# Decode attention on one core: value loads issued from ScalarE's queue instead of SyncE's

## The chip, the cores and the metric

The kernel runs on one core of a Trainium2 chip. The core has TensorE (PE, matrix products into PSUM), VectorE (DVE), ScalarE (ACT), GpSimd (POOL) and SyncE (SP), and 16 DMA engines that move data between the chip's memory and the core's SBUF. A load is issued by an instruction in the program of one engine, and each issuing engine has a DMA queue of its own. The metric is the device time of one execution in microseconds (us), lower is better.

## The reference

Two branches, A and B, of single-token attention over a cache of 4096 positions, 32 heads of 128, a batch of 2; all in float32. B uses A's input x. The branches are mixed by a gate.

```python
q = (x @ wq).reshape(B, Sq, Hq, Dh).transpose(0, 2, 1, 3)        # Sq = 1, Hq = 32, Dh = 128
scores = einsum("bhqd,bhkd->bhqk", q, k_cache) * Dh ** -0.5       # k_cache: 2 x 32 x 4096 x 128
p = softmax(scores, axis=-1)
o = einsum("bhqk,bhkd->bhqd", p, v_cache)
branch = o.transpose(0, 2, 1, 3).reshape(B, Sq, Hq * Dh) @ wo
...
g = sigmoid((x * gate_w).sum(-1, keepdims=True))
out = g * branch_A + (1 - g) * branch_B
```

## The kernel before

The work is cut into 32 units: branch (A, B), batch (2), and eight groups of four heads. A unit needs one tile of keys and one of values, each 128 partitions x 16384 float32 (8 MB): four heads times 32 stretches of 128 positions lie on the partitions. Units 0 to 15 belong to A, 16 to 31 to B. The query and output weights (`wq`, `wo`) of a branch are 8 MB each too, so all loads together are 68 such tiles: 2 wq, 32 keys, 32 values, 2 wo.

Keys, both wq, the values of the last unit (31) and the wo of B take turns in two buffers (`kt`). The values of units 0 to 30 and then the wo of A share one buffer (`vt`).

What a unit does:

- `scores(u)` on DVE: multiply the keys in place by the query (L182), then sum over each head's 128 elements (L183) into `sc`, of which there are two buffers. For units 0 and 16 both steps are done in halves, and the key is loaded in halves.
- `soft(u)`: DVE takes the maximum (L188 to L192, the last writes `nm`); ACT computes the exponentials, four pieces into `pr` (L197) and one into `pp` (L200). `pr` has one buffer.
- `values(u)`: 100 of 128 positions of a partition are weighted on PE, in 25 matmuls with `pr` (for the last unit 112). The other 28 are scaled in place on POOL (L220) and ACT (L222), added up on POOL (L227), and one more matmul with `heads` (L232 as well) takes their sum in. After every second unit ACT copies the result out (L236) and PE folds it into `gat` (L240). After every eighth (7, 15, 23, 31), `outputs` copies and multiplies once more, ending in the copy to `rows` on ACT (L253).

`project(n)` forms the queries of a branch on PE (L160, L168) from wq. `finish(n)` normalises `rows` on DVE and forms `on`; for A it stands behind `soft(16)`. At the end PE multiplies `on` by both wo (L299 to L309).

The order of instructions on each engine is the order in which the program writes them: the scheduler is manual. An engine runs its instructions strictly in that order, and a DMA issue waits in its engine's program like any other instruction, until the buffer that it fills is free. The loop is:

```python
for u in range(NU):
    scores(u)
    soft(u)
    ...                                  # finish("A") at u == 16
    load_k(u + 2 ...)                    # wq B at u == 14; value 31 at u == 30; wo B at u == 31
    ...                                  # at u == 15 also project("B"), load_k(17)
    values(u)
    ...                                  # wo A at u == 30
    load_v(u + 1)
```

So a key's load can be issued once VectorE has summed the unit two before, and a value's load once the last reader of the one value buffer, the matmul with `heads`, is done. Before the change, all loads but the two small ones into `raw` (x and gate_w, from ACT) are issued by SyncE, in this one sequence.

## Time and profile before

| | |
|---|---|
| median of 3 runs | 1325.07 us (1324.8 to 1325.48) |
| span of the profiled execution | 1324.0 us |
| read from memory | 570.43 MB |
| mean rate over the span | 431 GB/s |
| busy: PE, DVE, ACT, POOL | 407.2, 1129.4, 167.0, 369.0 us |

The profiled execution's own time is its span; it is 1.07 us under the median of the runs. In the page's lines, `Lnnn` is a line of the kernel, the engine and operation follow, then output<-input with shapes and the count; behind the bar stand the busy time, the mean in ns of one, and the idle time just before these instructions with what ended most of it. In a line of the timeline, the first number is the start and the second the duration in us; brackets give the engine's idle time before it and who ended it. SPq and ACTq are the issues of loads in the programs of SyncE and ScalarE; q1 is SyncE's DMA queue and q10 ScalarE's.

### The profile page before, as it was taken

To read this page: it belongs to the slowest core of one execution; us is meant where nothing else is said; L and a number is where in the kernel's file an instruction comes from. 1 tells how busy PE (TensorE), PEld (TensorE's weight loads), DVE (VectorE), ACT (ScalarE), POOL (GpSimd) and SP (SyncE) were. 2 spreads that over 40 slices of the span, in tenths; PEclk is the share of its full clock that TensorE was granted. 3 is DMA by queue.
4 is the path that set the end of the run, shared out by engine and by line. 5 is a ranking of instruction groups with operands and counts; after the bars stand their busy time and mean duration, and the time that the engine had idled before them with its cause. 6 is when DMAs were issued, how large, how long until landed. Compare 5 with 4: busy or idle time off the path is not lost.

```text
span 1324.0 us, 5510 instructions
## 1 busy us (share of the span) xinstructions
PE 407.2 (31%) x2092; PEld 98.9 (7%) x2092; DVE 1129.4 (85%) x191; ACT 167.0 (13%) x601; POOL 369.0 (28%) x145
## 2 busy tenths in 40 slices
PE   3132213233231323322442123332313332221356
PEld 1000000000000000000111000000000000000012
DVE  0999989889988888998369999899888889988860
ACT  0011101110110111011111101110111111011110
POOL 0033113333311333331132123333123333311350
PEclk9666556666656666665865566666556666655668
DMA  9999999999999999999999999999999999999998
GB/s 411 445 426 428 442 436 424 440 436 424 440 436 430 436 436 432 434 434 432 427 441 434 434 438 430 426 440 436 426 440 434 428 438 432 434 436 430 436 438 349
DMA packets 11124, 570.78 MB, mean 431 GB/s; under 512 B 1237, under 2 KB 1493, under 8 KB 1754
## 3 DMA queue, kind: packets, MB, share of 16 engines
q1 hardware_dynamic: 11092, 570.43, 99.6%
q8 instruction: 16, 0.26, 0.1%
q14 instruction: 10, 0.08, 0.0%
q10 hardware_dynamic: 6, 0.01, 0.0%
HBM read 570.43 MB, written 0.00 MB: 431 GB/s over the span
## 4 chain that ended last, share of the span: by engine, by line
DVE 50%; DMA 49%; PE 0%; issue 0%; SPq 0%; DVEq 0%
DVE sc L183 25%; DVE kt L182 25%; DMA kt<-in_A_k_cache_dram 25%; DMA kt<-in_B_k_cache_dram 22%; DMA kt<-in_B_wo_dram 3%; PE small L263 0%; DVE rm L188 0%; PE q L309 0%; SPq L89 0%; DVE tm L190 0%; DVE nm L192 0%; DVE rows L260 0%; SPq L79 0%; DVEq L183 0%; DVEq L336 0%
## 5 line engine op out<-in xcount | busy, mean ns | idle before, releaser
L182 DVE TENSOR_TENSOR kt<-kt,q 128x16384 f32<-128x16384 f32 (+1 forms) x34 | 551.3, 16215 | 131.9 <-DMA kt<-in_B_k_cache_dram 70.8
L183 DVE TENSOR_REDUCE sc<-kt 128x128 f32<-128x16384 f32 (+1 forms) x34 | 551.3, 16216 | 3.2
L232 PE MATMUL vp<-vt,pr 128*32 128x512 f32 x1550 | 258.7, 783 | 718.7 <-DMA vt<-in_A_v_cache_dram 379.5
L220 POOL TENSOR_TENSOR vt<-vt,pp 128x2560 f32<-128x2560 f32 x31 | 138.4, 4465 | 884.8 <-DMA vt<-in_A_v_cache_dram 468.3
L227 POOL TENSOR_TENSOR vt<-vt 128x1536 f32<-128x1536 f32 (+2 forms) x93 | 219.5, 2361 | 7.3
L222 ACT ACTIVATE vt<-vt,pp 128x128 f32<-128x128 f32 x248 | 75.9, 388 | 565.2 <-DMA vt<-in_A_v_cache_dram 291.3
L232 PEld LDWEIGHTS vp<-vt,pr 128*32 128x32 f32 x1550 | 68.2, 139 | 926.3 <-issue 920.7
L197 ACT ACTIVATE pr<-sc,nm 32x100 f32<-32x100 f32 (+1 forms) x128 | 59.9, 468 | 323.1 <-DVE nm L192 294.9
L232 PE MATMUL vp<-vt,heads 128*32 128x512 f32 x62 | 53.7, 965 | 108.9 <-POOL vt L227 108.9
L240 PE MATMUL gat<-vs,strip 128*32 128x512 f32 x32 | 29.8, 1032 | 11.0 <-ACT vs L236 11.0
L236 ACT ACTIVATE vs<-vp 128x512 f32<-128x512 f32 x16 | 9.6, 597 | 178.7 <-PE vp L232 178.7
L160 PE MATMUL small<-kt,xs 128*32 128x512 f32 x128 | 19.3, 758 | 17.0 <-DMA kt<-in_A_wq_dram 10.7
L197 ACT ACTIVATION_READ_ACCUMULATOR pr<-sc,nm 32x1 f32 x128 | 24.0, 187 | 0.0
L316 DVE COPY vs<-q 2x128 f32<-2x128 f32 x2 | 0.6, 282 | 23.5 <-PE q L309 23.5
L232 PEld LDWEIGHTS vp<-vt,heads 128*32 128x32 f32 x62 | 5.2, 130 | 137.1 <-POOL vt L227 137.1
L257 DVE RECIPROCAL rl<-rows 32x2 f32<-32x2 f32 x2 | 0.3, 148 | 15.8 <-ACT rows L253 15.8
L263 PE MATMUL small<-rows,deal 32*128 32x64 f32 x16 | 3.9, 418 | 29.0 <-DVE rows L260 29.0
L299 PE MATMUL q<-vt,on 128*2 128x512 f32 x64 | 9.1, 735 | 4.1 <-DMA vt<-in_A_wo_dram 4.1
L200 ACT ACTIVATE pp<-sc,nm 128x28 f32<-128x28 f32 (+1 forms) x32 | 10.2, 317 | 0.9
L188 DVE TENSOR_REDUCE rm<-sc 128x1 f32<-128x128 f32 x32 | 9.2, 286 | 1.1
L232 PE MATMUL vp<-kt,pr 128*32 128x512 f32 x56 | 7.7, 711 | 5.8 <-DMA kt<-in_B_v_cache_dram 5.8
L168 PE MATMUL q<-vs,spread 128*128 128x512 f32 x16 | 7.9, 618 | 3.0 <-ACT vs L164 3.0
(65 smaller groups left out, 88.1 us busy)
## 6 DMA issues: line engine op xcount, KB each, us to landing
kt<-in_A_k_cache_dram SPq DMA_DIRECT2D x2, 4096.0 KB, 35.7
kt<-in_B_k_cache_dram SPq DMA_DIRECT2D x2, 4096.0 KB, 38.3
kt<-in_B_wo_dram SPq DMA_DIRECT2D x1, 4096.0 KB
kt<-in_B_wo_dram SPq DMA_DIRECT2D x3, 1024.0 KB, 37.8
kt<-in_B_wo_dram SPq DMA_DIRECT2D x1, 512.0 KB, 40.4
vt<-in_A_v_cache_dram SPq DMA_DIRECT2D x16, 25.0
kt<-in_B_wo_dram SPq DMA_DIRECT2D x1, 256.0 KB, 40.5
kt<-in_B_wo_dram SPq DMA_DIRECT2D x2, 128.0 KB, 29.7
```

What stands on the lines that cost most here:

```text
L160: nc.tensor.matmul(r[h * QP:(h + 1) * QP], xs[:, c], cols[:, c, h, half * HG // 2:(half + 1) * HG // 2, :], start=c == 0, stop=c == KC - 1)
L182: nc.vector.tensor_tensor(k, k, q[:, None, :].to_broadcast([P, j - i, DH]), op=ALU.mult)
L183: nc.vector.tensor_reduce(sc[u][:, i:j], k, axis=AX.X, op=ALU.add)
L188: nc.vector.tensor_reduce(rm[:, 0:1], sc[u], axis=AX.X, op=ALU.max)
L197: nc.scalar.activation(w, sc[u][r, :spe].rearrange("p (c a) -> p c a", a=VC), AF.Exp, bias=nm[r], accum_out=lsum[r, g * HU + h:g * HU + h ...
L200: nc.scalar.activation(pp[u], sc[u][:, spe:], AF.Exp, bias=nm, accum_out=lpool[:, g:g + 1])
L220: nc.gpsimd.tensor_tensor(w[:, :m], w[:, :m], pp[u][:, :m, None].to_broadcast([P, m, DH]), op=ALU.mult)
L222: nc.scalar.activation(w[:, t], w[:, t], AF.Copy, scale=pp[u][:, t:t + 1])
L227: nc.gpsimd.tensor_tensor(x, x, y, op=ALU.add)
L232: nc.tensor.matmul(o[s * QP:(s + 1) * QP], w, x, start=not odd and c < STRIPS, stop=odd and c >= len(calls) - STRIPS)
L236: nc.scalar.activation(vs, o, AF.Copy)
L240: nc.tensor.matmul(gat[n, b][r:r + QP], strip, vs, start=True, stop=True)
```

## The change

The value loads of units 1 to 30 are issued from ScalarE. The loads of keys, of wq and wo, and of the values of units 0 and 31 stay on SyncE. The function's other lines, the buffers and the arithmetic are the same.

```diff
@@ -72,7 +72,8 @@
             vt[u] = big.tile([P, SLOTS, DH], F32, name="vt", bufs=1)
         else:
             vt[u] = big.tile([P, SLOTS, DH], F32, name="kt")
-        nc.sync.dma_start(vt[u], cache("v", u))
+        queue = nc.scalar if 0 < u < NU - 1 else nc.sync
+        queue.dma_start(vt[u], cache("v", u))
 
     def load_wq(n):
         wq[n] = big.tile([P, KC, H * DH], F32, name="kt")
```

Line numbers behind this place are one higher in the changed kernel.

First place: ScalarE's program around the end of a batch, units 6 and 7 and the beginning of 8, before the change. `vt_534` is the value tile of unit 6, `vt_592` of 7, `vt_665` of 8.

```order
L222 ACTIVATE vt_534<-vt_534,pp_549 128x128 x8
L197 ACTIVATE pr_88,lsum_90<-sc_594,nm_601 32x25x4 x4
L200 ACTIVATE pp_607,lpool_92<-sc_594,nm_601 128x28
L222 ACTIVATE vt_592<-vt_592,pp_607 128x128 x8
L236 ACTIVATE vs_652<-vp_553 128x512
L246 ACTIVATE vs_655<-gat_296 128x512
L253 ACTIVATE rows_663<-small_657 32x129
L197 ACTIVATE pr_88,lsum_90<-sc_667,nm_674 32x25x4 x4
L200 ACTIVATE pp_680,lpool_92<-sc_667,nm_674 128x28
```

The same place after the change:

```order
L223 ACTIVATE vt_534<-vt_534,pp_549 128x128 x8
L76 DMA vt_592<-in_A_v_cache_dram 128x16384
L198 ACTIVATE pr_88,lsum_90<-sc_594,nm_601 32x25x4 x4
L201 ACTIVATE pp_607,lpool_92<-sc_594,nm_601 128x28
L223 ACTIVATE vt_592<-vt_592,pp_607 128x128 x8
L237 ACTIVATE vs_652<-vp_553 128x512
L247 ACTIVATE vs_655<-gat_296 128x512
L254 ACTIVATE rows_663<-small_657 32x129
L76 DMA vt_665<-in_A_v_cache_dram 128x16384
L198 ACTIVATE pr_88,lsum_90<-sc_667,nm_674 32x25x4 x4
L201 ACTIVATE pp_680,lpool_92<-sc_667,nm_674 128x28
```

A value load now stands between the work on one unit's values and the exponentials of the next; at the end of a batch it stands behind the copy to `rows`.

Second place: SyncE's program at the seam of the branches, before. `kt_977` is the key of unit 15, `vt_1020` the value of 14, `kt_1098` the key of 16 in its halves, `kt_1147` the key of 17.

```order
L68 DMA kt_977<-in_A_k_cache_dram 128x16384
L75 DMA vt_1020<-in_A_v_cache_dram 128x16384
L79 DMA kt_1037<-in_B_wq_dram 128x16384
L75 DMA vt_1078<-in_A_v_cache_dram 128x16384
L68 DMA kt_1098<-in_B_k_cache_dram 128x8192 x2
L68 DMA kt_1147<-in_B_k_cache_dram 128x16384
L75 DMA vt_1199<-in_B_v_cache_dram 128x16384
```

After:

```order
L68 DMA kt_977<-in_A_k_cache_dram 128x16384
L80 DMA kt_1037<-in_B_wq_dram 128x16384
L68 DMA kt_1098<-in_B_k_cache_dram 128x8192 x2
L68 DMA kt_1147<-in_B_k_cache_dram 128x16384
L68 DMA kt_1229<-in_B_k_cache_dram 128x16384
```

The values between the keys are gone from the sequence. On TensorE, whose order is the same before and after, the projection of B (L160, L168) stands between the values of units 14 and 15:

```order
L232 MATMUL vp_1039<-vt_1020,pr_88 32x512 x25
L232 MATMUL vp_1039<-vt_1020,heads_94 32x512
L160 MATMUL small_1101<-kt_1037,xs_115 32x512 x16
L168 MATMUL q_1120<-vs_1118,spread_102 128x512
L168 MATMUL q_1122<-vs_1118,spread_102 128x512
L160 MATMUL small_1124<-kt_1037,xs_115 32x512 x16
```

The first two rows are the values of unit 14; nothing moved here.

Third place: SyncE's program at the end, before. `kt_2010` is the key of unit 31, `vt_2053` the value of 30, `kt_2070` the value of 31.

```order
L68 DMA kt_1952<-in_B_k_cache_dram 128x16384
L75 DMA vt_1993<-in_B_v_cache_dram 128x16384
L68 DMA kt_2010<-in_B_k_cache_dram 128x16384
L75 DMA vt_2053<-in_B_v_cache_dram 128x16384
L75 DMA kt_2070<-in_B_v_cache_dram 128x16384
L85 DMA vt_2111<-in_A_wo_dram 128x16384
L89 DMA kt_2131<-in_B_wo_dram 128x8192
```

After:

```order
L68 DMA kt_1952<-in_B_k_cache_dram 128x16384
L68 DMA kt_2010<-in_B_k_cache_dram 128x16384
L76 DMA kt_2070<-in_B_v_cache_dram 128x16384
L86 DMA vt_2111<-in_A_wo_dram 128x16384
L90 DMA kt_2131<-in_B_wo_dram 128x8192
```

The values of units 29 and 30 left the sequence; the value of 31, wo A and wo B keep their order behind the last key, and wo A still takes the buffer that the value of 30 leaves.

## The prediction

> **What bounds the kernel now.** I read the busy line first, then the DMA line and its queues, then the groups, the timeline of two units, and the two places where the pattern breaks (branch seam and end). All times are us.

> ```profile
> span 1324.0 us, 5510 instructions
> ...
> PE 407.2 (31%) x2092; PEld 98.9 (7%) x2092; DVE 1129.4 (85%) x191; ACT 167.0 (13%) x601; POOL 369.0 (28%) x145
> ...
> DMA  9999999999999999999999999999999999999998
> GB/s 411 445 426 428 442 436 424 440 436 424 440 436 430 436 436 432 434 434 432 427 441 434 434 438 430 426 440 436 426 440 434 428 438 432 434 436 430 436 438 349
> ...
> q1 hardware_dynamic: 11092, 570.43, 99.6%
> ...
> L182 DVE TENSOR_TENSOR kt<-kt,q 128x16384 f32<-128x16384 f32 (+1 forms) x34 | 551.3, 16215 | 131.9 <-DMA kt<-in_B_k_cache_dram 70.8
> ```

> The 16 DMA engines are never idle: one queue, q1, occupies 99.6% of the span. VectorE is busy 85% and its 131.9 of waiting is for keys. So the span is bytes over rate, and any stretch in which the DMA has nothing to do is added to it one for one. The change moves no bytes. What it can change is when loads become issuable, hence the DMA's idle time, now 0.4% of 1324, some 5.

> Two whole units of the steady state:

> ```profile
> 1005.58 0.33 SPq L75 DMA_DIRECT2D vt<-in_B_v_cache_dram  x1
> ...
> 1010.75 0.27 ACT L253 ACTIVATE rows<-small 32x129 f32<-32x129 f32 x1 [2.00 <-PE small L250]
> ...
> 1030.43 2.45 ACT L222 ACTIVATE vt<-vt,pp 128x128 f32<-128x128 f32 x8 [17.14 <-DMA vt<-in_B_v_cache_dram]
> ...
> 1044.30 0.33 SPq L75 DMA_DIRECT2D vt<-in_B_v_cache_dram  x1
> 1045.61 0.33 SPq L68 DMA_DIRECT2D kt<-in_B_k_cache_dram  x1
> ...
> 1046.46 0.47 ACT L197 ACTIVATE pr<-sc,nm 32x100 f32<-32x100 f32 x1 [13.58 <-DVE nm L192]
> ...
> 1048.64 0.19 ACT L200 ACTIVATION_READ_ACCUMULATOR pp<-sc,nm 128x1 f32 x1
> 1049.63 17.22 DVE L182 TENSOR_TENSOR kt<-kt,q 128x16384 f32<-128x16384 f32 x1 [3.26 <-DMA kt<-in_B_k_cache_dram]
> ...
> 1066.95 17.22 DVE L183 TENSOR_REDUCE sc<-kt 128x128 f32<-128x16384 f32 x1
> 1069.03 2.45 ACT L222 ACTIVATE vt<-vt,pp 128x128 f32<-128x128 f32 x8 [20.20 <-DMA vt<-in_B_v_cache_dram]
> ...
> 1088.30 17.22 DVE L182 TENSOR_TENSOR kt<-kt,q 128x16384 f32<-128x16384 f32 x1 [3.34 <-DMA kt<-in_B_k_cache_dram]
> ```

> A key lands at 1049.63, a value at 1069.03, the next key at 1088.30: transfers go strictly one after another, 19.3 each, and a unit takes 38.6. The value buffer is single, so from landing (1030.43) to the next value's issue (1044.30) no value load can be outstanding: 13.9. What fills this hole is the key that stands in the same queue. Key and value issue 1.3 apart and alternate, because each waits its turn behind the other on SyncE:

> ```profile
> SPq L75 <- PE vp L232: 986.4, 30, 37.1
> ```

> SyncE sits 986.4 in 30 waits before value loads. In program order the next key stands behind each of them. That wait is what the change takes away from the keys.

> **How two queues share.** The start is the only place where two queues have work:

> ```profile
> 0.74 0.39 SPq L79 DMA_DIRECT2D kt<-in_A_wq_dram  x1
> ...
> 1.29 0.23 ACTq L96 DMA_DIRECT2D raw<-in_gate_w_dram  x1
> ...
> 10.39 0.61 PE L133 MATMUL small<-ident,raw 3*128 3x3 f32 x4 [10.39 <-DMA raw<-in_gate_w_dram]
> ...
> 22.81 6.50 PE L160 MATMUL small<-kt,xs 128*32 128x512 f32 x32 [10.67 <-DMA kt<-in_A_wq_dram]
> ...
> 67.84 17.22 DVE L182 TENSOR_TENSOR kt<-kt,q 128x16384 f32<-128x16384 f32 x1
> ...
> 103.02 17.21 DVE L182 TENSOR_TENSOR kt<-kt,q 128x16384 f32<-128x16384 f32 x1
> ...
> kt<-in_A_wq_dram SPq DMA_DIRECT2D x1, 21.9
> raw<-in_gate_w_dram ACTq DMA_DIRECT2D x1, 2.0 KB
> ```

> **The change part by part.** The 30 issues (0.33 each, 10 in all) leave SyncE and go to ScalarE, which is 13% busy; in the steady state it then waits for scores or values, so they cost nothing. GpSimd issues no loads. The added wait there, for the last matmuls on vt, holds back the next unit's exponentials; these come after the scores (1046.46, against the value's issue at 1044.30), so it is free as long as VectorE is not ahead. At a batch's end the value load now also stands behind the rows copy: 1010.75 + 0.27 against 1005.58, 5.4 late, at units 7, 15 and 23.

> What matters is the order. Keys are now held by VectorE alone and want one per 35.2. They take 19.3 of it; the values get the remaining 15.9 per 35.2, so one value per 19.3/15.9 x 35.2 = 42.7. Values fall back 7.5 per unit until VectorE is stopped: scores have two buffers, so L183 of unit u+2 must follow the exponentials of u, which on ScalarE stand behind the issue of value u (some 3 from the issue: maximum and transpose are long done, exponentials 1046.46 to 1048.83). Now that L183 starts 1066.95 - 1005.58 = 61.4 after value u's issue, so there are 58 of slack, used up in 58/7.5 = 8 units. From then on keys lead by about one and a half units. The idle DMA that this makes:

> 1. *The end, 33.* On SyncE the loads of unit 31's value, wo A, wo B follow the last key, and wo A waits for values(30) since it takes vt. With the lead, key 31 and value 31 are in before value 29 is; then values(29) and values(30) each run with nothing to load: 2 x (13.9 + 2.6). The rows below show the present cover: wo A issues at 1275.94 while value 31 is still under way (landing 1281.65), and one transfer of 19.3 later, at 1300.93, its matmuls begin.

> ```profile
> 1275.94 0.33 SPq L85 DMA_DIRECT2D vt<-in_A_wo_dram  x1
> ...
> 1281.65 3.61 POOL L220 TENSOR_TENSOR kt<-kt,pp 128x2048 f32<-128x2048 f32 x1 [0.23 <-DMA kt<-in_B_v_cache_dram]
> ...
> 1296.89 0.23 DVE L266 COPY on<-small 128x64 f32<-128x64 f32 x1 [2.10 <-PE small L263]
> ...
> 1300.93 9.14 PE L299 MATMUL q<-vt,on 128*2 128x512 f32 x64 [4.07 <-DMA vt<-in_A_wo_dram]
> ```

> 2. *The seam, 21.* wq B and key 16 are in before value 14 lands; key 17 waits for the projection, whose matmuls stand on TensorE behind values(14). So values(14) runs with nothing to load: 16.4. Then value 15 and key 17 load together (38.6 + 2.6 = 41), while key 18 waits for the scores of 16 and value 16 for values(15) with its outputs: about 46, 5 more. Now the projection (642.52 to 657) lies beside the loads of value 15 and key 16 (landing 672.22):

> ```profile
> 642.52 5.55 PE L160 MATMUL small<-kt,xs 128*32 128x512 f32 x32 [6.30 <-DMA kt<-in_B_wq_dram]
> ...
> 655.13 1.98 PE L168 MATMUL q<-vs,spread 128*128 128x512 f32 x4 [0.78 <-ACT vs L164]
> ...
> 672.22 8.69 DVE L182 TENSOR_TENSOR kt<-kt,q 128x8192 f32<-128x8192 f32 x1 [32.98 <-DMA kt<-in_B_k_cache_dram]
> ```

> 3. *Units held by the score buffers, 12.* One pair of units by the half-rate rule, with the 2.6 split evenly: value u issues at 0, its bytes run 1.3 to 20.6; L183 runs 3 to 20.2, key issues 20.2, bytes from 21.5 (0.9 idle); values end 35.8; the second value's bytes start 37.1 and share with the key's last 3.7 until 44.5; the next key issues at 56.0 and shares 57.3 to 62.9; values end 78.1, and the pair repeats. Against 2 x 38.6 = 77.2 that is 0.9; with the 2.6 all ahead of the first byte it is nearer 1.7. Nine such pairs (units 8 to 14 and 19 to 29): 8 to 15; I take 12.

> 4. *Batch ends at 7 and 23, 8.* 0 to 5.4 each, by whether a key is in flight during the delay; in the pair above it mostly is not when an odd unit's values end (the key there finished at 79.4), so 4 each. (15 lies in the seam.)

> 5. *Units in which keys still run free, 10.* A value pass that meets a finished key leaves a gap; 35.2 and 42.7 come round once in 35.2/7.5, about 5 units, so twice in each branch. A gap is between 0 and 5 (the key rarely misses by more than a third of the 16.4); 4 x 2.5.

> Sum: 33 + 21 + 12 + 8 + 10 = 84. Span 1324.0 + 84 = 1408; the median of the runs is 1.07 above this profiled span, so 1409. Lower end of the terms 33 + 16 + 8 + 0 + 0 = 57, upper 33 + 21 + 15 + 11 + 20 = 100: 1382 to 1425. If the sharing is not even but keys get somewhat more, values fall back sooner and the gaps grow; I allow 10 for that.

> [...]

> **Rivals.** *Not slower: whole transfers alternate.* Key, value, key, value then come in the order of now, and the keys get no lead. It decides if the switch comes only after all 8 rows that an engine has of a load. Price 0 to 3 (a first value issued a little sooner or later): 1325 to 1328. For it: both loads are alike in size and always queued; against: 10.39 lies before 22.81. 0.08. *Values first.* If ScalarE's queue is preferred, a value takes 21.9 + 13.9 = 35.8, less than 38.6, and never falls back. Then value 30 passes key 31, whose scores end 19.3 later; wo A's matmuls have 1300.93 - 1297.12 = 3.8 to spare, so 15.5 to 19.3: 1343. Against: the gate load waited 8.9. 0.05. *Faster: two queues move more.* The best slice has 445 GB/s against 570.43 MB/1324 = 431; even all at 445 (1282) with the 84 comes to 1366. Only above 570.43/1240 = 460 would it be faster, which no slice reaches. 0.03. *Keys preferred*, more idle than my upper terms: above 1435. 0.04. The forecast: 0.80.

> **Numbers.** The range 1342 to 1435 holds the forecast with its allowance and most of values first, about 8 in 10; the forecast's own is 1382 to 1435. Slower by over 0.2% (about what a measurement of this kernel can tell from no change): 0.80 + 0.05 + 0.04 and 0.02 of the first rival, 0.91; within 0.06; faster 0.03.

> **What would show it.** Right: SyncE's 986.4 of value waits gone; the DMA line below 9 in the slice of the seam and in two near the end, its share about 93%; bytes unchanged, q10 carrying 30 of the 68 loads of 8 MB; value loads landing 22 to 40 after issue, where they now land 24.9 after (1030.43 against 1005.58); VectorE's L183 waiting for ScalarE from about unit 8, and its idle time for keys mostly gone; two matmul passes near the end 36 apart with no key load beside them. Wrong: a key and a value in flight together landing 19.3 apart (whole transfers), the DMA at 99% again, or a rate above 445.

## The result, and the profile after

The changed kernel takes 1429.69 us (median of 5 runs, 1427.08 to 1431.69) against 1325.07: 104.6 us longer, a ratio of 1.0788 with a 95% interval of 1.0775 to 1.0801. The prediction was 1409, within 1342 to 1435.

The lines of the changed kernel's page that answer to those shown of before; line numbers behind the change are one higher, so L183 and L184 are the two scoring steps:

```profile
span 1427.4 us, 5487 instructions
...
DMA  9999999999999999999598998999999999999558
GB/s 412 441 439 384 412 439 384 412 441 428 417 390 413 439 411 441 408 416 438 208 412 353 411 438 356 441 438 415 433 412 419 410 437 384 417 410 413 234 236 353
...
q1 hardware_dynamic: 6772, 318.77, 52.3%
q10 hardware_dynamic: 4326, 251.67, 41.4%
...
DMA vt<-in_A_v_cache_dram 34%; DMA vt<-in_B_v_cache_dram 29%; POOL vt L228 13%; POOL vt L221 8%; PE vp L233 3%; DMA kt<-in_B_wo_dram 3%; DMA kt<-in_A_wq_dram 2%; PE small L161 1%; ACT vt L223 1%; PE small L251 0%; PE gat L241 0%; SPq L90 0%; ACT vs L237 0%; PE q L169 0%; ACT vs L247 0%
...
L183 DVE TENSOR_TENSOR kt<-kt,q 128x16384 f32<-128x16384 f32 (+1 forms) x34 | 551.1, 16209 | 88.1 <-PE q L169 61.7
L184 DVE TENSOR_REDUCE sc<-kt 128x128 f32<-128x16384 f32 (+1 forms) x34 | 551.3, 16216 | 87.2 <-ACT pp L201 85.8
```

The bytes are the same (318.77 + 251.67 MB). The two queues together now take 93.7% of a longer span, where one took 99.6%. The chain that ended last used to go through VectorE and the key loads, as this line of before's page has it:

```profile
DVE sc L183 25%; DVE kt L182 25%; DMA kt<-in_A_k_cache_dram 25%; DMA kt<-in_B_k_cache_dram 22%; DMA kt<-in_B_wo_dram 3%; PE small L263 0%; DVE rm L188 0%; PE q L309 0%; SPq L89 0%; DVE tm L190 0%; DVE nm L192 0%; DVE rows L260 0%; SPq L79 0%; DVEq L183 0%; DVEq L336 0%
```

Now it is value load, value pass (the work on the value tile, L221 and L228), value load: 63% and 21%. VectorE waits for scores to be used up (L184, 85.8) and once for the projection (61.7), and for keys 26 in all, where it waited 131.9. SyncE's 986.4 of waiting before value loads is gone; it waits for VectorE instead:

```profile
SPq L68 <- DVE rm L189: 1098.9, 29, 47.9
```

Where the time went is read from the DMA's rate in seven stretches of the changed kernel (columns: stretch, length, busy time of each engine, clock, share of the DMA, GB/s):

```profile
0.00:320.00 320.00, 68.47 (x342) 17.00 (x342) 283.36 (x59) 29.62 (x106) 59.65 (x30) 0.62 0.98 419
320.00:684.00 364.00, 100.82 (x492) 23.29 (x496) 280.24 (x40) 46.18 (x170) 104.69 (x39) 0.58 0.98 415
684.00:802.00 118.00, 47.83 (x248) 13.53 (x247) 86.17 (x17) 16.75 (x59) 35.03 (x14) 0.66 0.80 338
802.00:950.00 148.00, 35.06 (x160) 7.80 (x160) 145.38 (x22) 15.21 (x56) 34.69 (x12) 0.57 0.97 418
950.00:1290.00 340.00, 86.64 (x434) 20.29 (x434) 294.91 (x43) 40.94 (x150) 93.00 (x34) 0.59 0.98 417
1290.00:1382.00 92.00, 32.56 (x168) 7.95 (x172) 35.39 (x7) 14.78 (x55) 36.72 (x15) 0.61 0.65 274
1382.00:1427.40 45.40, 28.64 (x256) 8.37 (x248) 1.99 (x7) 2.60 (x6) 5.58 (x3) 0.82 0.88 371
```

Two stretches of the kernel before, one from its units and its last one:

```profile
417.00:685.00 268.00, 92.65 (x454) 21.83 (x454) 217.06 (x32) 35.30 (x124) 81.30 (x30) 0.62 1.00 433
...
1290.00:1324.00 34.00, 22.00 (x205) 6.90 (x204) 1.99 (x7) 2.60 (x6) 0.00 (x0) 0.85 0.84 357
```

Each stretch loses (433 - rate)/433 of its length:

| stretch | what it is | lost, us |
|---|---|---|
| 0 to 320 | units with keys free, A | 10.3 |
| 320 to 684 | units held by the score buffers, A | 15.1 |
| 684 to 802 | the seam | 25.9 |
| 802 to 950 | keys free, B | 5.1 |
| 950 to 1290 | held, B | 12.6 |
| 1290 to 1427.4 | the end, 33.8 + 6.5, less the 6.0 of before's own end | 34.3 |

The sum is 103.3, and the two spans differ by 103.4. That they agree proves nothing yet: both kernels read the same bytes and 433 is before's rate, so the sum has to come out. The table shows where the time went; what it went into is in the trace's records of single rows (a row is the 64 KB of one partition, one record of 65536 bytes). The engines had no row under way for 89.5 us on average, against 5.4 before, so 84 of the 103 is time without work. The rest is rows that took longer, and most of that lies in the first 16 rows of a load, as many as there are engines: 2.69 us on average against 2.44 before, some 17 us of the span. All other rows take 2.42 in both kernels.

### The profile page after: what moved, and what is told of

Its sections match the earlier page's. It is cut to its first block, busy times and chain, and to the rows that moved or that the text cites. A ratio compares the mean times of both kernels' runs of the same rounds, so it can differ in the third digit from the quotient of the medians.

```text
span 1427.4 us, 5487 instructions
## 1 busy us (share of the span) xinstructions
PE 400.0 (28%) x2092; PEld 98.2 (7%) x2092; DVE 1127.4 (79%) x191; ACT 166.1 (12%) x601; POOL 369.4 (26%) x145
## 3 DMA queue, kind: packets, MB, share of 16 engines
q1 hardware_dynamic: 6772, 318.77, 52.3%
q10 hardware_dynamic: 4326, 251.67, 41.4%
HBM read 570.43 MB, written 0.00 MB: 400 GB/s over the span
## 4 chain that ended last, share of the span: by engine, by line
DMA 67%; POOL 21%; issue 5%; PE 5%; ACT 1%; SPq 0%; POOLq 0%; ACTq 0%
DMA vt<-in_A_v_cache_dram 34%; DMA vt<-in_B_v_cache_dram 29%; POOL vt L228 13%; POOL vt L221 8%; PE vp L233 3%; DMA kt<-in_B_wo_dram 3%; DMA kt<-in_A_wq_dram 2%; PE small L161 1%; ACT vt L223 1%; PE small L251 0%; PE gat L241 0%; SPq L90 0%; ACT vs L237 0%; PE q L169 0%; ACT vs L247 0%
## 5 line engine op out<-in xcount | busy, mean ns | idle before, releaser
L183 DVE TENSOR_TENSOR kt<-kt,q 128x16384 f32<-128x16384 f32 (+1 forms) x34 | 551.1, 16209 | 88.1 <-PE q L169 61.7
L184 DVE TENSOR_REDUCE sc<-kt 128x128 f32<-128x16384 f32 (+1 forms) x34 | 551.3, 16216 | 87.2 <-ACT pp L201 85.8
L233 PE MATMUL vp<-vt,pr 128*32 128x512 f32 x1550 | 253.8, 769 | 857.7 <-DMA vt<-in_A_v_cache_dram 453.1
L221 POOL TENSOR_TENSOR vt<-vt,pp 128x2560 f32<-128x2560 f32 x31 | 138.5, 4466 | 996.2 <-DMA vt<-in_A_v_cache_dram 539.2
L228 POOL TENSOR_TENSOR vt<-vt 128x1536 f32<-128x1536 f32 (+2 forms) x93 | 219.9, 2365 | 7.3
L317 DVE COPY vs<-q 2x128 f32<-2x128 f32 x2 | 0.6, 282 | 28.5 <-PE q L310 28.4
L191 DVE STREAM_TRANSPOSE tm<-rm 128x32 f32<-128x32 f32 x32 | 6.8, 212 | 1.1
## 6 DMA issues: line engine op xcount, KB each, us to landing
kt<-in_B_k_cache_dram SPq DMA_DIRECT2D x2, 4096.0 KB, 20.2
```

Source lines behind the costliest of these rows:

```text
L183: nc.vector.tensor_tensor(k, k, q[:, None, :].to_broadcast([P, j - i, DH]), op=ALU.mult)
L184: nc.vector.tensor_reduce(sc[u][:, i:j], k, axis=AX.X, op=ALU.add)
L221: nc.gpsimd.tensor_tensor(w[:, :m], w[:, :m], pp[u][:, :m, None].to_broadcast([P, m, DH]), op=ALU.mult)
L228: nc.gpsimd.tensor_tensor(x, x, y, op=ALU.add)
L233: nc.tensor.matmul(o[s * QP:(s + 1) * QP], w, x, start=not odd and c < STRIPS, stop=odd and c >= len(calls) - STRIPS)
```

## The experiments

Three theories stood. The order theory is that of the prediction: keys run ahead, values share the engines with them, and later value passes find no load beside them. The rate theory: two queues at once move fewer bytes per second. The place theory: a load issued from ScalarE stands behind ScalarE's work and starts late. All diffs are against the changed kernel; where an experiment has no interval, it ran once.

**Rate, read from the change itself.** Three stretches in which a value load is under way and a key load beside it for a part (the value issued at 149.12, for instance, is used from 184.71, 35.6 later):

```profile
152.00:183.00 31.00, 0.00 (x0) 0.00 (x0) 30.79 (x6) 0.00 (x0) 0.00 (x0) 0.50 1.02 440
200.00:228.00 28.00, 0.00 (x0) 0.00 (x0) 27.90 (x5) 0.84 (x4) 0.00 (x0) 0.50 1.03 442
300.00:324.00 24.00, 0.00 (x0) 0.00 (x0) 23.79 (x6) 0.00 (x0) 0.00 (x0) 0.50 1.01 437
```

They are no clean reading: from 200 to 214, for instance, the value is alone, and a stretch counts a row wholly where it begins, so short ones scatter (850 to 872 gave 432, and 900 to 922, shared throughout, 459). The records of the rows, counted by their own times, settle it: nine stretches in which both queues have rows under way throughout, 114 us in all, move 433 GB/s, as much as the kernel before. Sharing cost no rate here.

**All loads from ScalarE, one queue, old sequence.**

```diff
-            nc.sync.dma_start(kt[u][:, i:j], cache("k", u)[:, i:j])
+            nc.scalar.dma_start(kt[u][:, i:j], cache("k", u)[:, i:j])
...
-        queue = nc.scalar if 0 < u < NU - 1 else nc.sync
+        queue = nc.scalar
```

and the same for wq and wo.

> All loads, keys and weights too, issued from ScalarE in the old sequence, so that one queue holds them all. Order theory (keys run ahead and values share row by row, so that the DMA later stands idle): one queue keeps the old alternation, 1325 to 1330. Rate theory (two queues at once move fewer bytes per second): also 1325. Place theory (a value load issued from ScalarE stands behind ScalarE's work and starts late): as slow as the change or slower, 1400 or more.

Measured: 1338.74, ratio to before 1.0104 (1.0087 to 1.0121). Of the 104.6 all but 13.7 is gone, so the place alone isn't the cause. But the 13.7 is outside what I expected of the order theory, and I put it down to the place. About half of it (6.3 of the 12.1 by which the profiled spans differ) is there before the end: values are used as early as before up to unit 7, 2.4 later at unit 8, 5.3 later at unit 24 and 6.3 later at unit 31. The largest steps, 2.4 and 2.5, are at units 8 and 24, whose loads stand behind the last copies of a batch; unit 16, the third such place, has none. The rest arises at the end: the last two pieces of wo wait in ScalarE's program, and the copy of the last values waits behind them although the matmuls before it ended at 1297.

```profile
1288.41 19.08 ACTq L92 DMA_DIRECT2D kt<-in_B_wo_dram  x2
1296.06 1.02 PE L233 MATMUL vp<-kt,heads 128*32 128x512 f32 x2
1307.54 0.60 ACT L237 ACTIVATE vs<-vp 128x512 f32<-128x512 f32 x1 [20.51 <-DMA vt<-in_A_wo_dram]
```

In the change the loads of wo stayed on SyncE, so this end is no part of its loss.

**The mirror: values on SyncE, keys on ScalarE.**

```diff
-            nc.sync.dma_start(kt[u][:, i:j], cache("k", u)[:, i:j])
+            queue = nc.scalar if u > 1 else nc.sync
+            queue.dma_start(kt[u][:, i:j], cache("k", u)[:, i:j])
...
-        queue = nc.scalar if 0 < u < NU - 1 else nc.sync
+        queue = nc.sync
```

> The mirror: values back on SyncE, the keys of units 2 to 31 issued from ScalarE. Order theory: a key's issue now stands in ScalarE's program behind the work on the last values, so key and value are issued together, share the engines, land together, and each value pass has little to cover it; 30 passes of up to 16.4 with 8 to 11 uncovered: 1570 to 1660. Rate theory: the same two queues and bytes, 1430. Place theory: values are issued promptly again, 1325 to 1345.

Measured: 1670.89, 11 above my band. This run rules out the rate theory. It is no clean test of the place, since here it is the keys that wait in ScalarE's program, and the order theory too needs that wait, to tie a key to the last values. **Half of the change, every second value:**

```diff
-        queue = nc.scalar if 0 < u < NU - 1 else nc.sync
+        queue = nc.scalar if 0 < u < NU - 1 and u % 2 == 0 else nc.sync
```

> Only every second value (units 2, 4 to 30) from ScalarE, half of the change. Order theory: SyncE then waits before the odd values and holds the keys behind them as before, while the even ones share with a key; key and value land near each other and every second pass has no load beside it: 15 passes of 10 to 14 each: 1470 to 1530, more than the whole change costs. Rate and place theories: half of the 104, 1377.

Measured: 1525.89, within my band. Neither other theory lets half of the change cost 201 where the whole costs 105, or the mirror 346. What happens is plain in the mirror's timeline: the value is used from (L222) and the key from (L184) nearly the same time. The DMA is then empty until the next key, issued at 613.0, and the next value, issued at 617.5, share it and again finish together:

```profile
603.62 4.46 POOL L222 TENSOR_TENSOR vt<-vt,pp 128x2560 f32<-128x2560 f32 x1 [40.43 <-DMA vt<-in_A_v_cache_dram]
605.93 17.22 DVE L184 TENSOR_TENSOR kt<-kt,q 128x16384 f32<-128x16384 f32 x1 [24.18 <-DMA kt<-in_A_k_cache_dram]
...
649.25 17.22 DVE L184 TENSOR_TENSOR kt<-kt,q 128x16384 f32<-128x16384 f32 x1 [7.99 <-DMA kt<-in_A_k_cache_dram]
654.26 4.46 POOL L222 TENSOR_TENSOR vt<-vt,pp 128x2560 f32<-128x2560 f32 x1 [38.84 <-DMA vt<-in_A_v_cache_dram]
```

In the one queue of before, a value and a key issued 1.3 apart (1044.30 and 1045.61) are used 19.3 apart (1069.03 and 1088.30), and the second covers the pass of the first. In the mirror's two queues the key and the value issued 4.5 apart are used 5.0 apart, the value last, and its pass has neither of them left beside it.

**The lead: one score buffer, and three.**

```diff
-        sc[u] = work.tile([P, SLOTS], F32, name="sc")
+        sc[u] = work.tile([P, SLOTS], F32, name="sc", bufs=1)
```

> The change with one score buffer instead of two. Order theory: VectorE is stopped one scoring pass sooner, so the keys' lead is at most about half a unit instead of one and a half; one of the two uncovered value passes at the end goes and the seam shrinks: 1360 to 1395. Rate and place theories: nothing of theirs changes, 1430, or more if the lost buffer costs.

Measured: 1398.7, 31 less than the change, just above my band. By the reckoning of the table above the end loses 18 there instead of 34, and the seam 11 instead of 26: the 31 are saved where the lead had cost.

```diff
-        sc[u] = work.tile([P, SLOTS], F32, name="sc")
+        sc[u] = work.tile([P, SLOTS], F32, name="sc", bufs=3)
...
-        rm = work.tile([P, QP], F32, name="rm")
+        rm = work.tile([P, 1], F32, name="rm")
...
-        tm = work.tile([P, QP], F32, name="tm")
+        tm = work.tile([P, QP], F32, name="tm", bufs=1)
...
-        nm = work.tile([P, 1], F32, name="nm")
+        nm = work.tile([P, 1], F32, name="nm", bufs=3)
```

> The change with three buffers for the scores and for the negated maximum instead of two (the maximum's tile is narrower and the transposed one single, to make room). Order theory: VectorE may run one more unit ahead, so that one more value pass finds nothing to load at the end and one more at the seam, 2 x 16.4 on top of 1430, less what the longer free stretch saves: 1445 to 1465. If the lead is not what costs (rate or place theory), more freedom for VectorE changes nothing or helps: 1430 or less.

Measured: 1464.34, 35 more than the change. More freedom for VectorE makes the kernel slower and less makes it faster, as only the order theory has it. At the end of the kernel with three buffers there are three value passes beside which nothing is loaded, where the change has two:

```profile
1332.25 4.46 POOL L221 TENSOR_TENSOR vt<-vt,pp 128x2560 f32<-128x2560 f32 x1 [23.91 <-DMA vt<-in_B_v_cache_dram]
1346.06 0.33 ACTq L76 DMA_DIRECT2D vt<-in_B_v_cache_dram  x1
1367.82 4.46 POOL L221 TENSOR_TENSOR vt<-vt,pp 128x2560 f32<-128x2560 f32 x1 [23.82 <-DMA vt<-in_B_v_cache_dram]
1380.91 0.33 ACTq L76 DMA_DIRECT2D vt<-in_B_v_cache_dram  x1
1402.85 4.46 POOL L221 TENSOR_TENSOR vt<-vt,pp 128x2560 f32<-128x2560 f32 x1 [23.27 <-DMA vt<-in_B_v_cache_dram]
```

The two values issued there land 21.8 and 21.9 after their issue, that is, alone.

**Branch A only, branch B only.** The condition is `0 < u < per_branch` in one, `per_branch <= u < NU - 1` in the other.

> Only the values of units 1 to 15 from ScalarE, all of branch B's from SyncE. Order theory: the loss of branch A's units (about 25 by the rate in that stretch) and one pass of 16.4 at the seam or just behind it, where the lead has to be given back; no loss at the end: 1360 to 1375. Rate theory: half of the 104, 1377. Place theory: about half too, 1377, spread evenly.

> Only the values of units 16 to 30 from ScalarE. Order theory: the loss of branch B's units (about 18) and the two uncovered passes at the end (33), none at the seam, less a few because the lead starts from nothing: 1370 to 1382, with the two slices of about 235 GB/s at the end as in the change. Rate and place theories: 1377, without a concentration at the end.

Measured: 1369.24 and 1387.45. The two losses, 44 and 62, add up to 106 against 104.6. The first is where I had it. The second is 5 above my band, with the end as in the change: 269 GB/s for the 91 us ahead of wo, against 274 for 92.

**The batch ends.** The next value is issued before the batch's last copies on ScalarE:

```diff
+            if u < NU - 2:
+                load_v(u + 1)
             if g == HG - 1:
                 outputs(n, b)
...
-        elif u < NU - 2:
+        elif u < NU - 2 and u % 2 == 0:
             load_v(u + 1)
```

> The change with the next value's load issued before the batch-end copies (ScalarE's L247 and L254) instead of behind them, at units 7, 15 and 23. By the prediction's fourth term the delay of 5.4 there costs 0 to 5.4 each: 3 x 5.4 = 16 at most. Order theory: values are the late chain, so most of it counts: 1414 to 1422. If the keys cover the delay: 1430.

Measured: 1431.78, ratio to before 1.0793 (1.0774 to 1.0811), against 1.0788 (1.0775 to 1.0801): no gain. At unit 7 the value is issued at 419.62 and used from 444.06, 24.4 later; in the change it is issued at 423.09 and used from 445.17, 22.1 later. Of 3.5 earlier 1.1 is left.

**Who gets how much: the size of the rows.** Keys in quarters of their columns, so that a row is 16 KB beside the values' 64 KB:

```diff
-        for i, j in parts(u):
-            nc.sync.dma_start(kt[u][:, i:j], cache("k", u)[:, i:j])
+        for i in range(0, SLOTS, SLOTS // 4):
+            nc.sync.dma_start(kt[u][:, i:i + SLOTS // 4], cache("k", u)[:, i:i + SLOTS // 4])
```

> The change with each key loaded by four transfers of a quarter of its columns, so that a row is 16 KB for keys and 64 KB for values. Order theory with row-wise alternation: while both queues hold work a value gets four fifths instead of half, hardly falls back, and most of the idle time goes: 1343 to 1365. If the queues share by bytes or by whole transfers, the row's size changes nothing: 1430. Rate and place theories: 1430.

Measured: 1409.48, ratio 1.064 (1.0624 to 1.0656): 20 less than the change, where I expected 65 to 87. **The values in quarters** (the same cut in `load_v`, for those from ScalarE):

> The change with each value from ScalarE loaded by four transfers of a quarter of its columns (rows of 16 KB beside the keys' 64 KB). Row-wise alternation: a value gets a fifth while a key is in flight, lands later and falls back faster; the lead at the end is limited by the score buffers as before, so the loss is in the units: 1450 to 1530. Sharing by bytes, rate and place theories: 1430, plus a few for 90 more issues.

Measured: 1542.93, 13 above my band. **Both in quarters:**

> The change with keys and the values from ScalarE both loaded by quarters, so that both queues' rows are 16 KB and shares are even again. The held pairs lost 3 to 4 each where the prediction's hand cycle had 1.3. If the missing 2 to 3 are waits of a joining load for 64 KB rows under way, quarter rows take most of it away, 8 or 9 pairs by 2 to 3: 1405 to 1415. If they come from the even sharing itself: 1427 to 1435.

Measured: 1506.71, ratio 1.1384 (1.1364 to 1.1404), above both of my bands. As times these three can't be read simply, because more transfers bring a wait that I had left out: with five or eight transfers to a unit a key's issue waits until an earlier value has landed. Why it does, no run shows; the waits themselves are on record. In the change no key's issue waits for a value; with the values in quarters it does for 1058:

```profile
SPq L68 <- DMA vt<-in_B_v_cache_dram: 560.9, 13, 56.5
SPq L68 <- DMA vt<-in_A_v_cache_dram: 496.7, 14, 42.4
```

With the keys in quarters it is 287, with both 469. That couples keys to values somewhat as in the mirror. What can be read is the first value that meets a key in flight, that of unit 1, since up to there no key's issue has waited for a value, and the key beside it starts at nearly the same time in all four (first row between 105.8 and 106.8). The change:

```profile
94.66 0.36 ACTq L76 DMA_DIRECT2D vt<-in_A_v_cache_dram  x1
...
135.24 4.47 POOL L221 TENSOR_TENSOR vt<-vt,pp 128x2560 f32<-128x2560 f32 x1 [42.63 <-DMA vt<-in_A_v_cache_dram]
```

Keys in quarters:

```profile
94.84 0.37 ACTq L76 DMA_DIRECT2D vt<-in_A_v_cache_dram  x1
...
123.42 4.47 POOL L221 TENSOR_TENSOR vt<-vt,pp 128x2560 f32<-128x2560 f32 x1 [30.62 <-DMA vt<-in_A_v_cache_dram]
```

Both in quarters:

```profile
94.75 1.80 ACTq L78 DMA_DIRECT2D vt<-in_A_v_cache_dram  x4
...
136.20 4.46 POOL L223 TENSOR_TENSOR vt<-vt,pp 128x2560 f32<-128x2560 f32 x1 [43.49 <-DMA vt<-in_A_v_cache_dram]
```

From issue to use: 40.6 with equal rows of 64 KB, 41.5 with equal rows of 16 KB, 28.6 when the key's rows are a quarter of the value's, and 46.1 the other way round (four issues from 94.05 to 102.2, used 140.18). As an estimate from the 19.3 and the 2.6, an equal share makes the value's 19.3 take twice as long while a key is there, four fifths a quarter longer, 19.3 x 1.25 + 2.6 = 26.7. That fits rows begun in turn from the two queues, whatever their size, and the records have about as many of the one as of the other. Rows begun in a stretch with both queues at work: in the change, from 109 to 129, 73 of the value and 64 of the key; with the keys in quarters, from 110 to 119, 47 of 64 KB and 48 of 16 KB; with the values in quarters, from 107 to 127, 96 of 16 KB and 103 of 64 KB.

**Both remedies: one score buffer and keys in quarters.**

> The change with both remedies: one score buffer (1399 alone) and keys in quarters (1409 alone, against 1430). Order theory: the first caps the lead, the second slows its growth; if they add, 1430 - 31 - 20 = 1379, and with the lead no longer reaching its cap somewhat better: 1365 to 1380. Rate and place theories: near 1430 or no better than either alone.

Measured: 1373.54, 56 less than the change, where the two alone bring 31 and 20. It is still 48 slower than one queue. No version here beats the kernel before: its DMA was already busy 99.6% of the span.

## Why the prediction was right, and where it was off

**Bytes over rate, and idle DMA on top: right, for 84 of the 103.4.** The five terms were 84 of idle DMA, and the engines' idle time grew by 84. By term, in idle time alone, the end is 33 (33 forecast), the seam 25 (21), the held units 13 (12), and the units with keys free together with the batch ends 12 (18). That misses cancel so well is luck. What the prediction put at nothing is the longer first rows, 17. A load that comes to an empty queue was given 2.6 only where it found the DMA idle; before the change, and with all loads on ScalarE, the one queue nearly always held the next load, and first rows took 2.44 and 2.45. So 1429.69 lies above the upper sum of the terms, 1425. It is inside the forecast's own range because of the 10 allowed for keys getting more than half, which they did not: that too is luck. Why a first row takes longer, no run shows.

**Half the rate each: right.** It rested on one row, the gate load that got in under four rows. The row-size runs show it for large loads, so whole-transfer alternation (the first rival) and a preferred queue (values or keys first) are out. Whole transfers in turn would have given 19.3 + 2.6 plus the rest of the key for unit 1's value and no change with the size of rows; the measured 40.6 and 28.6, and the 73 and 64 rows begun from 109 to 129, decide against that. The shared stretches move before's 433 GB/s, so the second queue brought no rate.

**The lead grows to a limit at about unit 8: right, with a step off.** The first L184 that waits for ScalarE is that of unit 8 (342.51, after 5.4 of waiting). But the values fell back faster than the prediction had it: the issues of units 1 to 6 are 49 apart on average (94.66 to 339.69), not 42.7. By its own count, 8 units of falling back and a wait two units ahead, the limit would have come later. That the unit is right is partly luck.

**The end, 33: right, 34.3.** Values 29 and 30 of the changed kernel run their passes bare, with no load beside them, 1332.25 to 1346.09 and 1368.09 to 1381.88:

```profile
1332.25 4.47 POOL L221 TENSOR_TENSOR vt<-vt,pp 128x2560 f32<-128x2560 f32 x1 [28.73 <-DMA vt<-in_B_v_cache_dram]
...
1346.09 0.34 ACTq L76 DMA_DIRECT2D vt<-in_B_v_cache_dram  x1
1368.09 4.47 POOL L221 TENSOR_TENSOR vt<-vt,pp 128x2560 f32<-128x2560 f32 x1 [24.07 <-DMA vt<-in_B_v_cache_dram]
...
1381.88 0.33 SPq L86 DMA_DIRECT2D vt<-in_A_wo_dram  x1
```

**The seam, 21: 25.9.** Value 14's bare pass and the projection behind it are there (VectorE's 61.7 for the query). The other gap, forecast at 5, is at the pass of value 16: that value has landed at 779.68, and the next key can be issued only when VectorE has summed unit 17, at 786.4. For 8.6 in all the engines have no row. Both passes, by the last two numbers, the share of the DMA and its GB/s:

```profile
684.00:698.00 14.00, 10.67 (x62) 2.70 (x65) 0.00 (x0) 2.29 (x8) 11.43 (x4) 0.74 0.00 1
...
780.00:787.00 7.00, 7.00 (x48) 1.91 (x41) 6.90 (x4) 2.06 (x8) 6.92 (x2) 0.70 0.00 0
```

**Units held by the score buffers, 12: mis-sized, 27.7 (15.1 + 12.6).** Of the five terms this one was furthest off. Of the 27.7, 13 is idle DMA, as forecast; 11 is the longer first rows, which the hand cycle does not have; and about 4 of the whole belongs to units 6 and 7 (320 to 423), where the wait for the scores has only begun. The hand cycle gave 78.1 for a pair. Seven pairs, from the issue of one value to that of the second after it (units 8 to 14 and 21 to 29), take 77.5 to 81.4, 79.1 on average. One of the longest:

```profile
1188.22 0.34 ACTq L76 DMA_DIRECT2D vt<-in_B_v_cache_dram  x1
...
1210.54 4.47 POOL L221 TENSOR_TENSOR vt<-vt,pp 128x2560 f32<-128x2560 f32 x1 [24.05 <-DMA vt<-in_B_v_cache_dram]
...
1224.40 0.33 ACTq L76 DMA_DIRECT2D vt<-in_B_v_cache_dram  x1
...
1255.74 4.47 POOL L221 TENSOR_TENSOR vt<-vt,pp 128x2560 f32<-128x2560 f32 x1 [33.40 <-DMA vt<-in_B_v_cache_dram]
...
1269.57 0.33 ACTq L76 DMA_DIRECT2D vt<-in_B_v_cache_dram  x1
```

The lone value takes 22.3 (22 in the cycle), but the one that shares takes 31.3 where the cycle had 28.4, and the pair 81.4. The cycle lets a joining load have its half at once, 1.3 after its issue, and its landing follow 1.3 behind its last byte. The trace has two waits in their place. From the issue at 1224.40 to 1228.5 only rows of the key are begun, 31 for the 16 engines; the value's first rows begin 4.1 to 5.9 after the issue. The DMA queues from 1224.5 to 1228.5 (packets, MB, share):

```profile
q1 hardware_dynamic: 31, 2.03, 117.4%
```

And the value's last row ends 28.3 after the issue, at 1252.68, but its use begins 3.1 later. In between (1252.7 to 1255.7) the engines begin 16 rows of the next key and one packet of 4 bytes of the value's queue:

```profile
q1 hardware_dynamic: 16, 1.05, 80.6%
q10 hardware_dynamic: 1, 0.00, 0.0%
```

So this value was used only after 16 more rows of the other queue. In 17 of the 30 value loads 32 to 34 key rows, two for each engine, begin between the start of the value's last row and the use, and the use comes 2.9 to 3.2 after that row's end; in the other 13 at most 16 do, and the use comes 0.4 to 0.6 after. With rows of 16 KB in the key it is 1.1, for the value of unit 1 in both of those runs. The gate load, quoted for the half rate, had waited 8.9 for a row of 2 KB; I used it for the share and not for the delay. The run with both in quarters was to show these waits as time; its other waits prevent that.

**Batch ends, 8: nothing to be seen.** Issuing earlier there brought no gain, to within some 4 us by the two intervals.

**Units with keys free, 10: 15.4 (10.3 + 5.1), of it 12 idle, whatever of the batch ends is in it.** The count was guessed, and the size is of that order.

**Issues cost nothing: not contradicted for these loads.** The delay at the batch ends cost nothing in the change, where keys are ahead; it cost about 2.5 each at units 8 and 24 in the run with all loads on ScalarE, where the loads of wo cost time as well.

**More rate, hence faster: out.** Whole slices reach 441 at best, against the 460 needed.

## What to carry to other kernels

When the DMA is the bound, ask of a second queue not what it adds but which order it takes away. A wait in a shared queue may be what keeps two streams in step: here SyncE's 986 us of waiting cost nothing and held the keys where each of them covered a value's pass. And two loads that shared landed nearly together (used 5.0 apart in the mirror, 19.3 in one queue), so with a single buffer behind one of them nothing was left to load while it was used; the run with half of the change, slower than the whole, shows how far this goes.

## What the runs showed of the hardware that was not expected

- In these runs the bytes that each queue got followed the size of its rows: the same value took 28.6, 40.6 or 46.1 us from issue to use beside a key of smaller, equal or larger rows (in the last case the value itself was cut).
- In the change a value load had rows of the key ahead of it at both ends: its first rows begun 4.1 to 5.9 us after the issue in the load shown, and its use 2.9 to 3.2 us after its last row in 17 of 30 loads, where it was 0.4 to 0.6 in the 13 with at most 16 key rows in between.
- The first rows of a load took 2.69 us on average in the change, where a load mostly came to an empty queue, and 2.44 in the kernel before, whose one queue nearly always held the next load; why, no run shows.
- A load that waited in ScalarE's program held that engine's later work: with all loads issued there, the copy behind wo's last pieces ran at 1307.54, about 10 us after its input was there (1297), and the kernel's end lost about 6.
- Cutting loads into quarters brought waits of its own: 1058 us of key issues waiting for values to land. The 113 us that cutting the values cost the whole kernel (1542.93 against 1429.69) are these waits and the values' smaller share together.
